# Linear attention and a highway layer on one core: all engine orders replaced, two decay factors made by products, the last pieces written another way

## The chip, the cores and the metric

One core of one Trainium2 chip runs the kernel. Its engines are TensorE (PE; its weight loads are PEld), VectorE (DVE), ScalarE (ACT), GpSimd (POOL) and SyncE (SP), which issues the loads and stores. Each engine takes its instructions in the order in which they are written and waits, in that order, for what each needs. The metric is the device time of one execution in microseconds (us), lower is better.

## The reference, cut to what matters

Inputs are q, k, v of 4 batches, 8 heads, 768 positions and 64 channels, a decay `lam` per head, two weights of 512 x 512 and a bias, all float32.

```python
for b in range(nb):                       # blocks of 64 positions, per head
    intra = (qb @ kb.T) * Dmask           # lam ** (i - j) where i >= j, else 0
    out[b] = intra @ vb + (qb * lam ** (pos + 1)) @ kv_state
    kv_state = lam ** 64 * kv_state + (kb * lam ** (63 - pos)).T @ vb
x = out.transpose(0, 2, 1, 3).reshape(3072, 512)
H = maximum(x @ w_h, 0)
T = sigmoid(x @ w_t + b_t)
result = T * H + (1 - T) * x
```

## The kernel before

The 4 x 768 positions are cut into twelve tiles n of 256 rows, three to a batch; a tile has two blocks b of 128 rows. The decay is split: v is multiplied by `lam ** -t` (`pow_v`, step CV), and the attention's result by `lam ** t` (`pow_o`, step D), so that scores need only a mask of zeros and ones (`tri`), and the state `kv` is a plain sum in PSUM. `pow_o` has three parts, one for each place of a tile in its batch, `[128, 2, 4, 128]` each; step `PW.i` makes part i, as four exponentials on ACT.

The whole order of the program is written by hand in the string `PLAN`: one token for one step, `name.tile.block...@engine=bank`. The steps:

- loads on SP, half a tile of q, k or v each (256 KB): `Lq`, `Lk`, `Lv`; the weights by `W` (half a matrix, 512 KB, `W.1` is w_t and `W.0` is w_h); stores `ST` of a tile (512 KB), in parts for the last tile
- casts to bf16: `CK`, `CQ` (a third number 2 means the whole tile, 0 or 1 a half), `CV` with the factor, `WC` of the weights
- transposes on PE (`TK`, `TQ`, `RK`, `RQ`, `RKF`, `RQF`) and their copies out of PSUM (`EK`, `EQ`, `FK`, `FQ`)
- scores `S`, state `U`, both interleaved `SA`, `SB`; mask `M` on DVE; state to bf16 `KE`; attention `A` (inside the block) and `I` (with the state); result to bf16 `D` on DVE
- the highway layer for 128 rows and 512 columns (a last number 0 or 1 means 256 columns, used for tile 11, block 1): `BP` copies the bias into a PSUM bank, `F.n.b.1` adds the gate's matmuls to it, `F.n.b.0` makes relu's input; `TX`, `TXB` transpose the rows back and `XC` copies them out as `xs`; `H` = max(h, 0) - x on DVE; `G` the sigmoid on ACT, in place in PSUM or (`@S`) into SBUF; `X` the product with the gate; `Y` the sum with x, into the output buffer `ob`
- `Z.r` runs r matmuls that only keep PE busy; `QB`, `RB` spread the bias; `PT` loads ACT's sigmoid table

Before PLAN's steps a set-up makes the identity, the masks, `ln` of the decays, `off` (ln times the start of each part, on POOL) and `pow_v`. Buffers are rings (`BUFS`: four of each load, four of `ob`, six of `y`, three of `g`); a load into a buffer waits until the last step that reads it is done, and SP holds everything behind it.

Of the kernel before, what the change touches and what calls it, by code (L numbers as in the profile page):

```python
# [21 lines left out]
Lk.2.1 WC.1.1.0@ACT WC.1.1.1@POOL S.1.0=14 D.0.1@DVE KE.0.1@ACT WC.1.0.1@POOL Lq.3.0 BP.0.1.2@DVE=0 PT F.0.0.1.2
M.1.0.1 Lq.3.1 CV.1.2@POOL M.1.1.1 TXB.0.0=3 G.0.0.2@S F.0.1.1.2 Lk.3.1 M.1.1.0 Z.2=6 M.1.0.0 G.0.1.2@S U.1.0 Lk.3.0
WC.0.1.0@POOL A.1.1=52 BP.1.0.2@DVE=0 KE.1.0@ACT TXB.0.1=4 WC.0.1.1@POOL Lv.2.1 A.1.0 BP.1.1.2@ACT=6 I.1 CQ.2.2@DVE
XC.0.2.1@ACT U.1.1 D.1.0@DVE RQF.2=1 Lv.2.0 WC.0.0.1@ACT WC.0.0.0@POOL F.1.0.1.2 EQ.2.1@DVE XC.0.2.0@ACT D.1.1@DVE
Lv.3.0 EQ.2.0@ACT F.0.1.0.2=4 CK.2.2@DVE Lv.3.1 TXB.1.1=3 TXB.1.0=5 H.0.1.2 Lq.4.0 XC.1.2.1@ACT RKF.2=1 F.0.0.0.2=2
KE.1.1@ACT X.0.1.2@POOL EK.2.1@DVE Lq.4.1 XC.1.2.0@ACT EK.2.0@DVE S.2.0=31 G.1.0.2@S H.0.0.2 Lk.4.0 CQ.3.2@POOL
S.2.1=45 F.1.1.0.2=0 M.2.1.1 Lk.4.1 CK.3.2@ACT Y.0.1.2@POOL M.2.0.1 RQF.3=5 Lv.4.1 M.2.0.0 RKF.3=2 EQ.3.1@ACT M.2.1.0
F.1.0.0.2=4 Lq.5.0 EK.3.1@ACT CV.2.2@POOL H.1.1.2 EK.3.0@ACT S.3.1=31 Lq.5.1 H.1.0.2 EQ.3.0@ACT F.1.1.1.2 M.3.1.1
BP.2.0.2@ACT=0 Lv.4.0 CV.3.2@POOL U.2.0 M.3.0.1 S.3.0=25 Lk.5.0 KE.2.0@ACT A.2.0=14 M.3.0.0 A.2.1 I.2 Lk.5.1  # L30
CQ.4.2@ACT M.3.1.0 X.0.0.2@POOL U.3.0 D.2.0@DVE Lv.5.0 A.3.1=32 G.1.1.2 A.3.0 D.2.1@DVE RQF.4=5 KE.3.0@ACT Lv.5.1
CK.4.2@POOL F.2.0.1.2 EQ.4.0@DVE X.1.1.2@DVE Lk.6.0 I.3 Y.0.0.2@POOL G.2.0.2@S RKF.4=1 EQ.4.1@DVE Lk.6.1 D.3.0@DVE
F.2.0.0.2=4 EK.4.0@ACT D.3.1@DVE Lq.6.0 CQ.5.2@POOL EK.4.1@ACT TX.2.2=56 U.3.1 XC.2.2.0@ACT Lq.6.1 S.4.1=01
Y.1.1.2@DVE CV.4.2@POOL TXB.3.0=3 XC.2.2.1@ACT RQF.5=5 M.4.0.1 Lv.6.1 KE.3.1@ACT TXB.3.1=2 F.3.0.0.2=6 H.2.0.2
XC.3.2.0@ACT Lq.7.1 EQ.5.1@ACT M.4.1.1 CK.5.2@POOL F.2.1.0.2=0 XC.3.2.1@ACT H.3.0.2 Lv.6.0 EQ.5.0@ACT X.1.0.2@POOL
BP.3.0.2@DVE=4 SA.4=3 RKF.5=1 Lq.7.0 KE.4.0@ACT M.4.1.0 F.3.0.1.2 BP.2.1.2@ACT=6 CV.5.2@POOL EK.5.1@DVE Lk.7.0
# [39 lines left out]
def kernel(  # L76
# [82 lines left out]
    for i in range(1, NST):  # L159
        P.tensor_scalar(off[:, i], in0=off[:, 0], scalar1=float(2 * C * i), scalar2=None, op0=ALU.mult)  # L160
# [313 lines left out]
```

## Time and profile before

| | before |
|---|---|
| time, median of 3 runs | 103.34 us (101.49 to 103.61) |
| profiled execution: its time, its span | 102.99 us, 101.3 us |
| PE busy | 91.9 us (91% of the span) |
| DVE busy | 85.7 us (85%) |
| POOL busy | 82.3 us (81%) |
| ACT busy | 74.5 us (74%) |
| DMA | 27.54 MB, mean 272 GB/s |
| HBM | 20.97 MB read, 6.29 MB written |

The span runs from the first to the last instruction of the profiled execution; the time of that execution has something around it. Busy time is that of instructions at work: a waiting instruction isn't counted, and the ends of matmuls are modelled, so that PE's share says least. Where a row of a group ends with "idle before", this is the time that its engine waited ahead of such instructions, and the arrow names what ended most of it. In a row of the timeline the first number is the start and the second the length, both in us.

### The profile page before, as it was taken

To read this page: it belongs to the slowest core of one execution; us is meant where nothing else is said; L and a number is where in the kernel's file an instruction comes from. 1 tells how busy PE (TensorE), PEld (TensorE's weight loads), DVE (VectorE), ACT (ScalarE), POOL (GpSimd) and SP (SyncE) were. 2 spreads that over 40 slices of the span, in tenths; PEclk is the share of its full clock that TensorE was granted. 3 is DMA by queue.
4 is the path that set the end of the run, shared out by engine and by line. 5 is a ranking of instruction groups with operands and counts; after the bars stand their busy time and mean duration, and the time that the engine had idled before them with its cause. 6 is when DMAs were issued, how large, how long until landed. Compare 5 with 4: busy or idle time off the path is not lost.

```text
span 101.3 us, 4242 instructions
## 1 busy us (share of the span) xinstructions
PE 91.9 (91%) x1784; PEld 57.0 (56%) x1803; DVE 85.7 (85%) x157; ACT 74.5 (74%) x134; POOL 82.3 (81%) x83
## 2 busy tenths in 40 slices
PE   5999999999889998999999897999999999999910
PEld 1445566565547764675676654685567474465700
DVE  4137749998979998999999985999899989999870
ACT  3596958886598599799898895869996673664610
POOL 6734557732969999998799998999899999999830
PEclk9999999999999999999999999999999999999995
DMA  0999999999999999999999999999999105009683
GB/s 22 309 300 311 357 338 365 366 340 302 254 292 306 338 300 290 299 271 304 283 288 288 319 314 395 392 310 279 294 392 364 36 6 201 6 21 366 239 307 112
DMA packets 33335, 27.54 MB, mean 272 GB/s; under 512 B 1443, under 2 KB 26275, under 8 KB 33316
## 3 DMA queue, kind: packets, MB, share of 16 engines
q1 hardware_dynamic: 33312, 27.27, 87.4%
q8 instruction: 14, 0.23, 1.0%
q14 instruction: 5, 0.04, 0.2%
q10 hardware_dynamic: 4, 0.00, 0.0%
HBM read 20.97 MB, written 6.29 MB: 269 GB/s over the span
## 4 chain that ended last, share of the span: by engine, by line
PE 31%; DMA 29%; SPq 10%; POOL 7%; DVE 7%; issue 7%; ACT 5%; DVEq 0%; POOLq 0%; ACTq 0%
DMA kf<-in_k_dram 14%; PE bt L378 9%; PE bh L378 9%; DMA w_f<-in_moe_w_h_dram 8%; DMA qf<-in_q_dram 7%; SPq L198 5%; SPq L194 4%; PE kv L267 2%; PE bs L262 2%; POOL ob L404 2%; POOL kb L113 2%; DVE y L391 2%; POOL vs L221 2%; PE bo L335 2%; SPq L202 2%
## 5 line engine op out<-in xcount | busy, mean ns | idle before, releaser
L304 DVE TENSOR_TENSOR m<-bs,tri 128x512 bf16<-128x512 f32 x48 | 31.0, 681 | 1.2 <-PE kv L267 1.0
L221 POOL TENSOR_TENSOR vs<-vf,pow_v 128x1024 bf16<-128x1024 f32 (+1 forms) x13 | 23.4, 1805 | 5.1 <-DMA vf<-in_v_dram 3.1
L378 PEld LDWEIGHTS <-xT 128*128 128x128 bf16 x200 | 17.7, 98 | 16.8 <-DVE xT L341 0.3
L404 POOL TENSOR_TENSOR ob<-y,xs 128x512 f32<-128x512 bf16 x21 | 24.3, 1173 | 0.6 <-DVE y L400 0.4
L378 PE MATMUL bh<-w_b,xT 128*128 128x512 bf16 (+1 forms) x93 | 23.8, 370 | 0.5
L378 PE MATMUL bt<-w_b,xT 128*128 128x512 bf16 (+1 forms) x89 | 23.1, 370 | 1.1 <-issue 0.3
L400 POOL TENSOR_TENSOR y<-g,y 128x512 bf16<-128x512 f32 x15 | 17.3, 1159 | 2.7 <-DVE y L391 2.6
L391 DVE SCALAR_TENSOR_TENSOR y<-bh,xs 128x512 bf16<-128x512 f32 (+1 forms) x25 | 16.3, 660 | 1.8 <-PE bh L378 1.8
L341 DVE TENSOR_TENSOR xT<-bo,pow_o 128x512 bf16<-128x512 f32 x24 | 15.6, 679 | 0.1
L111 ACT ACTIVATE ss<-kv 128x512 bf16<-128x512 f32 x19 | 11.4, 601 | 3.9 <-PE kv L267 3.8
L396 ACT ACTIVATE g<-bt 128x512 f32<-128x512 f32 x15 | 9.0, 602 | 5.0 <-PE bt L378 4.4
L111 ACT ACTIVATE bt<-b_bc 128x512 f32<-128x512 f32 (+1 forms) x20 | 11.5, 580 | 1.4 <-DVE xT L341 0.6
L262 PE MATMUL bs<-qT,kT 64*64 64x128 bf16 x384 | 11.5, 220 | 0.0
L111 ACT ACTIVATE xs<-bx 128x512 bf16<-128x512 bf16 x15 | 9.0, 604 | 1.3 <-PE bx L354 0.8
L262 PEld LDWEIGHTS <-kT 64*64 64x64 bf16 x384 | 8.2, 106 | 2.7 <-DVE kT L113 1.2
L267 PE MATMUL kv<-vs,kb 64*64 64x64 bf16 x320 | 8.6, 194 | 0.2 <-POOL vs L221 0.2
L267 PEld LDWEIGHTS <-kb 64*64 64x64 bf16 x320 | 7.0, 109 | 3.0 <-issue 2.0
L335 PE MATMUL bo<-m,vs 64*64 64x128 bf16 x384 | 8.5, 218 | 0.0
L418 PE MATMUL bspin<-blank,id 128*128 128x512 bf16 x26 | 8.3, 444 | 0.1
L113 POOL CAST kb<-kf 128x1024 bf16<-128x1024 f32 (+1 forms) x7 | 6.8, 976 | 1.5 <-DMA kf<-in_k_dram 1.5
L396 ACT ACTIVATE bt<-bt 128x512 f32<-128x512 f32 (+1 forms) x10 | 5.5, 546 | 2.4 <-PE bt L378 2.4
L335 PEld LDWEIGHTS <-vs 64*64 64x64 bf16 x384 | 6.4, 107 | 0.6
(67 smaller groups left out, 133.2 us busy)
## 6 DMA issues: line engine op xcount, KB each, us to landing
...
```

The source lines that it names most:

```text
L111: A.activation(dst, src, AF.Copy)
L221: ENG[eng].tensor_tensor(buf("vs", n)[:, hs], in0=buf("vf", n)[:, hs].rearrange("p h (j d) -> p h j d", j=J), in1=pow_v[:, n % NST, hs, :, ...
L262: T.matmul(get("s", n, e, hp // 2)[half(b), hp % 2, j, :], lhsT=buf("kT", n)[half(e), hp, j, half(b)], rhs=q_cols(n, half(e), hp, b), star ...
L267: T.matmul(kv[half(e), hp, half(e)], lhsT=buf("kb", n)[half(b), j, 2 * hp + e, :], rhs=buf("vs", n)[half(b), 2 * hp + e, j, :], start=firs ...
L304: V.tensor_tensor(buf("m", n, e, u), in0=get("s", n, e, u), in1=tri[:, None].to_broadcast([128, 2, J, C]), op=ALU.mult)
L335: T.matmul(get("o", n, b)[half(e), hp, :], lhsT=buf("vs", n)[half(b), 2 * hp + e, j, :], rhs=buf("m", n, e, hp // 2)[half(b), hp % 2, j, : ...
L341: V.tensor_tensor(cut(buf("xT", n)[:, :, b * C:(b + 1) * C]), in0=get("o", n, b).rearrange("e k (j p) -> e k p j", j=Q), in1=cut(pow_o[:, ...
L378: T.matmul(t, lhsT=buf("xT", n)[:, j, b * C:(b + 1) * C], rhs=w_b[w][:, j, z], start=(j == 0 and not w), stop=(j == KC - 1), skip_group_ch ...
L391: V.scalar_tensor_tensor(buf("y", n, b)[:, z], in0=get("h", n, b, p), scalar=0.0, in1=buf("xs", n)[:, b, z], op0=ALU.max, op1=ALU.subtract)
L396: A.activation(buf("g", n, b)[:, cols(p)] if to == "S" else t, t, AF.Sigmoid)
L400: ENG[eng].tensor_tensor(y, in0=buf("g", n, b)[:, cols(p)] if eng == "POOL" else get("t", n, b, p), in1=y, op=ALU.mult)
L404: ENG[eng].tensor_tensor(buf("ob", n)[:, b, z], in0=buf("y", n, b)[:, z], in1=buf("xs", n)[:, b, z], op=ALU.add)
```

## The change

Three things are changed.

1. `PLAN` is another order of all engines. On SP: `Lk` of tile 0 comes first, both halves of `Lv.1` stand ahead of the four `W` (before: behind the first two), `Lv.2` ahead of `Lq.3` and `Lk.3`, `ST.1` and `ST.2` between the loads of tiles 9 to 11, and `ST.4` behind `ST.6`. There are 20 `Z` matmuls in place of 27. Steps that change engine:

```
to DVE from POOL: CK.1.2 CK.5.2 CV.0.1 X.0.1 X.8.0
to DVE from ACT:  CK.3.2 CK.11.2 KE.1.1 PW.1 PW.2 BP.1.1 BP.3.1 BP.11.0 BP.11.1.0
                  EK.0.1 EK.3.1 EQ.1.0 EQ.3.1 FK.6.0 FK.6.1 FK.9.0 FQ.7.0 FQ.9.0 FQ.10.1
                  XC.0.0 XC.2.0 XC.2.1 XC.3.1 XC.7.0 XC.7.1
to POOL from DVE: CK.0.1 CQ.2.2 X.1.1 X.2.1 X.3.0 X.7.1 Y.1.1
to POOL from ACT: CK.8.2 CQ.4.2 WC.0.0.1 WC.1.1.0
to ACT from POOL: CK.4.2 CK.7.2 CK.9.2 CK.10.2 CQ.0.1 CQ.3.2 CQ.5.2 CQ.8.2 WC.0.0.0 WC.1.0.1
to ACT from DVE:  CQ.0.0 CQ.1.2 BP.0.1 BP.1.0 BP.3.0 BP.6.0 BP.9.1
                  EK.0.0 EK.2.1 EQ.0.1 EQ.2.1 EQ.4.0 FK.10.1 FQ.6.0 FQ.7.1 FQ.9.1 FQ.10.0 FQ.11.0 FQ.11.1
                  XC.4.1 XC.5.1 XC.10.0 XC.10.1 XC.11.0
```

2. Parts 1 and 2 of `pow_o` are products of part 0 with a factor per head, `grown`, on DVE; four plus four exponentials on ACT go, one small one comes.
3. The last two pieces (tile 11, block 1, 256 columns each) are computed as relu(h) g + (1 - g) x: `GN` makes 1 - g as a second sigmoid, `R` its product with x, `HG` relu(h) times g, and `Y` sums the two. Before they were g (relu(h) - x) + x.

```diff
 PLAN = """
-Lk.0.0 Lq.0.0 Lq.0.1 Lk.0.1 Lv.0.1 Lq.1.0 Z.9=5 Lq.1.1 PW.0@ACT CQ.0.0@DVE Lv.0.0 CK.0.0@POOL Lk.1.0 Lk.1.1
-CQ.0.1@POOL TK.0.0=2 W.1.0 PW.2@ACT Z.1=5 TQ.0.2=3 CK.0.1@DVE W.1.1 Z.1=5 TK.0.1=4 EQ.0.0@DVE QB=6 EQ.0.1@DVE Lv.1.0
-CV.0.1@POOL EK.0.0@DVE EK.0.1@ACT Lv.1.1 S.0.0=01 RB@ACT S.0.1=53 CQ.1.2@DVE Lq.2.1 Z.3=4 PW.1@ACT M.0.0.0 RQF.1=2
...
-Y.10.0.2@POOL F.11.1.0.0=5 G.11.0.2 TXB.11.1=3 F.11.1.1.0 X.11.0.2@DVE XC.11.2.1@ACT ST.10 F.11.1.0.1=0 G.11.1.0
-H.11.1.0 F.11.1.1.1 Y.11.0.2@POOL H.11.1.1 X.11.1.0@DVE G.11.1.1 X.11.1.1@DVE ST.11.0.2 Y.11.1.0@DVE Y.11.1.1@DVE
-ST.11.1.0 ST.11.1.1
+Lk.0.1 Lk.0.0 Lq.0.1 Lq.0.0 Lv.0.0 Lv.0.1 Z.5=1 Lq.1.0 PW.0@ACT Lq.1.1 CK.0.1@POOL Lk.1.0 CK.0.0@POOL Lk.1.1 TK.0.1=2 TK.0.0=3
+PW.2@DVE Lv.1.0 CQ.0.1@ACT Z.6=1 Lv.1.1 CQ.0.0@ACT PW.1@DVE EK.0.0@ACT TQ.0.2=4 W.1.1 Z.3=1 EQ.0.1@ACT EK.0.1@DVE CV.0.0@POOL
+Z.1=3 W.1.0 EQ.0.0@DVE PT S.0.1=60 S.0.0=15 CV.0.1@DVE W.0.1 QB=3 M.0.1.0 U.0.0 Z.2=4 W.0.0 CQ.1.2@ACT KE.0.0@DVE Lq.2.0
...
+F.11.1.1.0 F.11.1.0.0=6 XC.11.2.1@ACT X.11.0.2@DVE F.11.1.1.1 ST.10 G.11.1.0@S GN.11.1.0 F.11.1.0.1=5 Y.11.0.2@POOL
+HG.11.1.0 GN.11.1.1 R.11.1.0@DVE G.11.1.1@S R.11.1.1@DVE HG.11.1.1 ST.11.0.2 Y.11.1.0@DVE Y.11.1.1@DVE ST.11.1.0 ST.11.1.1
 """
...
+    grown = singles.tile([128, NST, NP], F32)
+    A.activation(grown[:, 1:], off[:, 1:], AF.Exp)
...
+    rest = singles.tile([C, DM], F32)
+    part = singles.tile([C, DM], F32)
+    parted = set()
...
-    def powers(i):
+    def powers(i, eng):
+        if eng != "ACT":
+            ENG[eng].tensor_tensor(pow_o[:, i], in0=pow_o[:, 0], in1=grown[:, i, None, :, None].to_broadcast([128, 2, NP, C]), op=ALU.mult)
+            return
...
+    def sigm_rest(n, b, p):
+        A.activation(rest[:, cols(p)], get("t", n, b, p), AF.Sigmoid, scale=-1.0)
+
+    def kept(n, b, p, eng):
+        z = cols(p)
+        ENG[eng].tensor_tensor(rest[:, z], in0=rest[:, z], in1=buf("xs", n)[:, b, z], op=ALU.mult)
+
+    def gated(n, b, p):
+        z = cols(p)
+        V.scalar_tensor_tensor(part[:, z], in0=get("h", n, b, p), scalar=0.0, in1=buf("g", n, b)[:, z], op0=ALU.max, op1=ALU.mult)
+        parted.add((n, b, p))
...
     def total(n, b, p, eng):
         z = cols(p)
-        ENG[eng].tensor_tensor(buf("ob", n)[:, b, z], in0=buf("y", n, b)[:, z], in1=buf("xs", n)[:, b, z], op=ALU.add)
+        last = (n, b, p) in parted
+        ENG[eng].tensor_tensor(buf("ob", n)[:, b, z], in0=part[:, z] if last else buf("y", n, b)[:, z],
+                               in1=rest[:, z] if last else buf("xs", n)[:, b, z], op=ALU.add)
```

More of the change, by code (lines that the diff above doesn't have):

```diff
@@ L22 @@
[L22 to L36, printed above, removed]
@@ L429 @@
         "KE": lambda a, e, bk: evac_s(*a, e), "M": lambda a, e, bk: mask(*a),
-        "I": lambda a, e, bk: inter(*a, bk), "A": lambda a, e, bk: intra(*a, bk), "D": lambda a, e, bk: take(*a, e), "PW": lambda a, e, bk: powers(*a), "QB": lambda a, e, bk: spread(bk), "RB": lambda a, e, bk: copy(e, b_bc, get("qb")),
+        "I": lambda a, e, bk: inter(*a, bk), "A": lambda a, e, bk: intra(*a, bk), "D": lambda a, e, bk: take(*a, e), "PW": lambda a, e, bk: powers(*a, e), "QB": lambda a, e, bk: spread(bk), "RB": lambda a, e, bk: copy(e, b_bc, get("qb")),
         "TX": lambda a, e, bk: rows(*a, bk), "TXB": lambda a, e, bk: rows_full(*a, bk),
```

35 lines of the change are left out of this document (2 added, 33 removed).

## The prediction, made before the changed kernel ran

> **What bounds the kernel now.** I read the busy line and the chain of the page first, then busy time by stretch, then the groups by form, then the timeline around single rows. In the first fence the reader is to see that four engines are nearly full, and that the chain which ended last is spread over all of them.
>
> ```profile
> PE 91.9 (91%) x1784; PEld 57.0 (56%) x1803; DVE 85.7 (85%) x157; ACT 74.5 (74%) x134; POOL 82.3 (81%) x83
> ...
> PE 31%; DMA 29%; SPq 10%; POOL 7%; DVE 7%; issue 7%; ACT 5%; DVEq 0%; POOLq 0%; ACTq 0%
> ```
>
> The stretches (columns: stretch, its length, then busy us and count of PE, PEld, DVE, ACT, POOL; granted clock; DMA share; GB/s) say where each engine has room.
>
> ```profile
> 0.00:10.10 10.10, 8.86 (x68) 4.17 (x69) 4.30 (x12) 6.57 (x14) 5.72 (x19) 1.00 0.78 235
> 10.10:15.00 4.90, 4.85 (x72) 2.93 (x74) 3.17 (x6) 3.88 (x9) 2.79 (x4) 1.00 1.12 349
> 15.00:30.00 15.00, 13.95 (x268) 8.59 (x259) 13.34 (x24) 11.69 (x21) 9.22 (x10) 1.00 1.08 323
> 30.00:95.00 65.00, 62.64 (x1386) 40.15 (x1395) 62.08 (x111) 50.92 (x91) 62.75 (x51) 1.00 0.87 266
> 95.00:101.30 6.30, 1.59 (x17) 1.20 (x14) 2.85 (x7) 1.48 (x4) 1.77 (x2) 0.79 0.59 212
> ```
>
> From 30 to 95 us, of 65.0 us, DVE is busy 62.08, POOL 62.75, PE 62.64 and ACT 50.92. A long stall of one engine is not there to be removed. DVE from 15 to 95 us is busy 13.34 + 62.08 = 75.42 of 80, so its waits are 4.6 us. Before 10.1 us it works only 4.30. DMA is behind this:
>
> ```profile
> 66.39 4.44 SPq L198 DMA_DIRECT2D vf<-in_v_dram  x4
> 70.87 25.15 SPq L408 DMA_DIRECT2D out_dram<-ob  x9
> ```
>
> The last four loads (tile 11's v among them) are issued by 70.83 us and the queue then holds only stores; 30 us of compute follow. So I take DVE as the bound: its end is its start, plus its work, plus its waits, with PE and POOL close behind. The span is 101.3 us, the profiled execution 102.99 us (1.69 us lie around the span); the median of the runs is 103.34 us, 0.35 more, and the runs go from 101.49 to 103.61, so that about 2% is what a measurement here can tell from no change.
>
> **The change part by part.** Prices, by operation and shape (mean ns of one is the number after the comma):
>
> ```profile
> L304 DVE TENSOR_TENSOR m<-bs,tri 128x512 bf16<-128x512 f32 x48 | 31.0, 681 | 1.2 <-PE kv L267 1.0
> ...
> L221 POOL TENSOR_TENSOR vs<-vf,pow_v 128x1024 bf16<-128x1024 f32 x11 | 21.3, 1943 | 2.8 <-DMA vf<-in_v_dram 1.9 <-DVE m L304 0.5 <-DMA qf<-in_q_dram 0.4
> L400 POOL TENSOR_TENSOR y<-g,y 128x512 bf16<-128x512 f32 x15 | 17.3, 1159 | 2.7 <-DVE y L391 2.6
> L113 POOL CAST kb<-kf 128x1024 bf16<-128x1024 f32 x6 | 6.2, 1038 | 1.5 <-DMA kf<-in_k_dram 1.5
> ...
> L346 ACT ACTIVATE pow_o<-t_f,off 128x256 f32<-128x256 f32 x12 | 5.7, 559 | 0.0
> L400 DVE TENSOR_TENSOR y<-bt,y 128x512 bf16<-128x512 f32 x8 | 5.4, 681 | 0.3 <-ACT bt L396 0.3
> L111 ACT ACTIVATE qb<-qf 128x1024 bf16<-128x1024 f32 x5 | 5.3, 1052 | 2.0 <-DMA qf<-in_q_dram 2.0
> ...
> L111 ACT ACTIVATE kb<-kf 128x1024 bf16<-128x1024 f32 x4 | 4.2, 1060 | 1.2 <-DMA kf<-in_k_dram 1.2
> ...
> L113 DVE COPY xs<-bx 128x512 bf16<-128x512 bf16 x9 | 3.6, 412 | 0.4 <-POOL ob L404 0.4
> L113 DVE COPY bt<-b_bc 128x512 f32<-128x512 f32 x5 | 3.4, 682 | 0.0
> ...
> L404 DVE TENSOR_TENSOR ob<-y,xs 128x512 f32<-128x512 bf16 x2 | 2.1, 1064 | 0.0
> ...
> L113 DVE CAST qb<-qf 128x512 bf16<-128x512 f32 x1 | 0.9, 887 | 0.7 <-DMA qf<-in_q_dram 0.7
> ...
> L404 DVE TENSOR_TENSOR ob<-y,xs 128x256 f32<-128x256 bf16 x2 | 0.7, 416 | 0.0
> L113 DVE CAST kb<-kf 128x1024 bf16<-128x1024 f32 x1 | 0.7, 694 | 0.4 <-DMA kf<-in_k_dram 0.4
> ...
> L113 DVE CAST kb<-kf 128x512 bf16<-128x512 f32 x1 | 0.4, 427 | 1.5 <-DMA kf<-in_k_dram 1.5
> ...
> L152 DVE TENSOR_TENSOR p_ln<-ln,tk_f 128x48 f32<-128x48 f32 x1 | 0.2, 209 | 1.4 <-ACT ln L150 1.4
> ```
>
> *Shared-port work.* DVE steps with two SBUF inputs, or SBUF to SBUF casts, have met POOL three times. In the rows below ob of 512 takes 0.84 and 1.29 where 0.681 is the time of such an operation; the half cast qb took 0.887 against 0.427 for kb:
>
> ```profile
> 36.59 0.84 DVE L404 TENSOR_TENSOR ob<-y,xs 128x512 f32<-128x512 bf16 x1
> 88.84 1.29 DVE L404 TENSOR_TENSOR ob<-y,xs 128x512 f32<-128x512 bf16 x1
> ```
>
> and POOL was held at the same two places (1.90 and 1.16 are its usual times):
>
> ```profile
> 36.84 2.35 POOL L221 TENSOR_TENSOR vs<-vf,pow_v 128x1024 bf16<-128x1024 f32 x1
> 89.67 1.49 POOL L404 TENSOR_TENSOR ob<-y,xs 128x512 f32<-128x512 bf16 x1
> ```
>
> So a meeting costs DVE 0.16 to 0.61 and POOL 0.3 to 0.4. Y.1.1's goes with the step (counted below); Y.8.0's 0.61 goes if its place is free: -0.61. But after 15 us the new order has five such steps on DVE (CK.2.2, 3.2, 5.2, 11.2, Y.8.0) beside a POOL that is 97% busy. Nothing but the order of each engine keeps them apart. Bounds: 0, and five times a whole vs product, 1.9. I take two meetings at 0.45, a middle price and what qb paid: +0.9.
>
> The Trainium skill, page "SBUF — State Buffer", section "Who interferes with whom", states that this pair of ports is an exclusive lock: whichever of the two engines starts first keeps it for its whole instruction. The rows agree: POOL's 2.35 row begins under DVE's 0.84 row and ends 0.44 late. Taken at its word, a cast that meets a fresh vs product would wait up to 1.9 us, and two such would be 3.8 for my 0.9; that is a rival below.
>
> *DVE after the start.* I counted the steps of both orders by engine. Leaving DVE: the cast CQ.2.2 (0.70, as the kb cast of that size, 0.694), five bias copies BP (5 x 0.682 = 3.41), four gates X (4 x 0.681 = 2.72), the two half gates of the last pieces (0.84 together, at the half ob's 0.416), Y.1.1 (0.84). Coming: casts CK.1.2, 3.2, 5.2, 11.2 (4 x 0.694 = 2.78), three BP and a half one (2.05 + 0.42), KE.1.1 (0.69, as a cast), two gates X (1.36), two half products R (0.84 together). Fifteen 0.41 us copies out of PSUM leave and fifteen come. 8.51 go, 8.14 come: -0.37 us. The H steps of the last pieces become HG at the same form.
>
> *Two decay factors as products.* Eight of the twelve exponentials leave ACT: 8 x 5.7/12 = -3.8 us. DVE gets two products of 1024 elements from two SBUF inputs. Not shown before: between 0.694 (the 1024-element cast) and 1.94 (the product of that size on POOL). From 48 elements in 0.209 and 512 in 0.681 a product costs 1.02 ns per element, so 1024 take 1.20; I take that, 2.4 in all. The first 10 us of DVE change by CQ.0.0, CQ.1.2, CK.0.1 and two copies leaving (0.89 + 0.70 + 0.43 + 0.83 = 2.85) and products, CV.0.1 (0.68) and one copy coming (3.5): +0.65, beside 5.8 idle us there.
>
> ```profile
> 4.41 3.67 ACT L346 ACTIVATE pow_o<-t_f,off 128x256 f32<-128x256 f32 x8
> 4.47 0.42 POOL L160 TENSOR_SCALAR off<-off 128x4 f32<-128x4 f32 x2
> ...
> 10.10 1.88 DVE L304 TENSOR_TENSOR m<-bs,tri 128x512 bf16<-128x512 f32 x3
> ```
>
> A wait is added: the new little exponential `grown` needs `off`, ready at 4.89, and stands ahead of PW.0 on ACT, which began at 4.41. With about 0.2 for `grown`, PW.0's four exponentials (3.67/8 = 0.46 each) end near 6.9 in place of 6.25. Queued behind are CQ.0.1, CQ.0.0, EK.0.0 and EQ.0.1 on ACT, and on DVE both products, EK.0.1, EQ.0.0, CV.0.1 and the first mask. Products end at 6.9 + 2.4 = 9.3, CV.0.1 and two copies later it is 10.8; the first mask ran at 10.10. So +0.7, at worst +1.7 with a port wait. DVE is idle 1.7 us in the 4.9 us after that (3.17 busy), which a later start eats first, and I count the start at 0; without that cover it is the 0.7.
>
> *Loads.* SP now takes both halves of v1 ahead of the four w loads (512 KB each), and v2 ahead of q3 and k3. The second half of w_t comes two 256 KB units later, 0.52 MB at the 349 GB/s of 10 to 15 us = 1.5 us.
>
> ```profile
> 16.28 0.82 PE L378 MATMUL bt<-w_b,xT 128*128 128x512 bf16 x3 [0.17 <-DVE xT L341]
> ```
>
> The first gate block, 16.28 us, moves to about 17.8 on PE; v1 comes four units, 3 us, earlier, so that the attention of tile 1 fills PE meanwhile. I cost it at nothing; uncovered it is 1.5. Stores: ST.1 and ST.2 now stand ahead of the last loads. Lv.11 waits on SP behind ST.2, thus for Y.2.1 on POOL and for one more 512 KB, 1.5 us at that rate; with 30 us left after the last load this costs nothing. ST.4 goes behind ST.6; Y.8 reuses its buffer only after five more POOL steps (over 6 us). Fewer warming matmuls (20 for 27) are no work on the path.
>
> *Tail.* Before, the last matmul group is the gate's, and sigmoid, gate and sum follow:
>
> ```profile
> 95.99 0.60 PE L378 MATMUL bt<-w_b,xT 128*128 128x256 bf16 x4
> ...
> 96.62 0.83 DVE L400 TENSOR_TENSOR y<-bt,y 128x256 bf16<-128x256 f32 x2
> 96.63 0.37 ACT L396 ACTIVATE bt<-bt 128x256 f32<-128x256 f32 x1 [0.44 <-PE bt L378]
> ...
> 97.37 0.75 DVE L404 TENSOR_TENSOR ob<-y,xs 128x256 f32<-128x256 bf16 x2
> ```
>
> From 96.59 it takes a sigmoid to 97.00, a gate to 97.45 and the sum to 98.12. After, relu's block is last; the sigmoid has begun one half block (0.43, four of its 256-wide matmuls) earlier, but GN precedes it (0.3). HG and two sums follow: 1.3 for 1.5. -0.2 us; R reads two SBUF inputs beside POOL's Y.11.0, which may take it back.
>
> *POOL and ACT.* POOL: five CK, one CQ (1.04 each) and CV.0.1 (1.04) fewer, two X (1.16) and one Y (taken as an X) more: -3.8 us. ACT: -3.8 for the exponentials, three CQ (1.05), one CK (1.06), two half CQ (half of 1.05 and a little, 0.6), one BP (taken as DVE's, 0.7), two half sigmoids GN (0.37) and `grown` more: about +3.2. From 15 to 95 us ACT is busy 11.69 + 50.92 = 62.6 of 80; 5 more fit.
>
> *Waits of DVE.* The order is new, so its 4.6 us of waits are drawn anew. Where before packs well, they are small:
>
> ```profile
> 30.00:40.00 10.00, 9.63 (x228) 6.70 (x224) 9.51 (x17) 8.33 (x16) 9.96 (x8) 1.00 1.12 305
> 40.00:50.00 10.00, 9.74 (x210) 5.80 (x211) 9.67 (x18) 8.96 (x16) 9.42 (x8) 1.00 1.01 292
> 50.00:60.00 10.00, 9.67 (x255) 6.70 (x256) 10.00 (x19) 8.82 (x16) 9.33 (x8) 1.00 1.02 295
> ```
>
> 0.49, 0.33 and 0.00 us in three tens, 0.27 in the mean; at that rate 80 us would have 2.2, a gain of 2.4. Lighter POOL speaks for some of it, fuller ACT against. Bounds -2.4 and +2.4; I take half the gain, -1.2.
>
> Sum: -0.37 - 0.61 + 0.9 - 0.2 - 1.2 = -1.5 us: 102.99 - 1.5 = **101.5 us**, in its own range 100.3 to 102.6.
>
> **The rivals.**
>
> *Good packing.* No new meetings and all of the 2.4: -0.37 - 0.61 - 0.2 - 2.4 = -3.6, 99.4 us. For it: POOL, 97% full, gets 3.8 us of room, and so every gate waits less. Against: PE's 62.64 of 65 has the same work.
>
> *PE or the balance binds.* PE's matmuls of the tiles are untouched; if it ends last in most stretches, DVE's saved work turns into waits: 102.99, call it 103.0. For: PE is the largest share of the chain, 31%. Against: its ends are modelled, so its share overstates.
>
> *Casts meet POOL.* The other side. The five steps after 15 us meet POOL, at 0.75 each, between the 0.61 measured and half a vs product, 0.95: 3.8 us; PW.1 or CV.0.1 meets CV.0.0 at the start and the first mask is 1.7 late with no cover. -0.37 - 0.2 + 3.8 + 1.7 - 0.6 (Y.8.0's own, paid already) = +4.3, but POOL's -3.8 gives back a share of its waits, 1.2: 106.1 us. It loses from about three meetings at the long price on. For: POOL is 97% full; both steps of 512 elements after 30 us met it. Against: five POOL casts fewer leave gaps. The exclusive lock on the page named above is this rival's mechanism.
>
> *The order does not do what it says.* Loads come at other moments than planned, the new order waits for w_t (1.5) at the head of PE and saves nothing else: 104.1.
>
> **How the numbers follow.** Forecast 0.42, good packing 0.26, PE binds 0.15, casts 0.11, late loads 0.06. Within the forecast's case some 0.4 lies more than 2% below the median (101.27), so faster is 0.26 + 0.16 = 0.42; over 105.4 lies the casts' case and a little of the last, 0.12; same 0.46. The range of 8 in 10 is 98.8 to 104.4: it takes in most of the fast case and the late loads, and leaves out the casts.
>
> **What would show it.** Right: DVE's sum about 85 us, POOL's near 78, ACT's near 78; kb casts on DVE at 0.69; first mask between 10 and 11 us; pow_o products near 1.2 us each; POOL's 2.35 row gone. Wrong: kb casts on DVE over 1 us, DVE waits over 5 us between 15 us and the end, or a first gate block after 19 us. A forecast of no net gain would show as PE full and DVE idle.

## The result: 3.4% slower, and the profile after

The changed kernel takes 105.74 us (median of 6 runs, 105.05 to 107.35), the kernel before 102.84 us on the same chip (6 runs, 101.49 to 103.61): a ratio of 1.034, with an interval from 1.025 to 1.044. The profiled execution took 105.05 us, its span is 103.3 us: 2.0 us over the 101.3 before. The forecast was 101.5. Medians are over all runs; ratios and their intervals are over the runs within 1.5% of a kernel's fastest, so that the two can differ.

The busy line and the shares of the chain that ended last, of the kernel after:

```profile
PE 91.3 (88%) x1778; PEld 56.8 (55%) x1796; DVE 90.0 (87%) x156; ACT 76.7 (74%) x136; POOL 79.4 (77%) x79
...
PE 76%; DVE 13%; issue 4%; ACT 3%; DVEq 0%; ACTq 0%
```

The reader is to see the last line first. Before, PE had 31% of the chain beside DMA's 29%; now the chain lies on PE for 76% of the span. POOL and ACT came out as counted (79.4 and 76.7 for "near 78"); DVE has 90.0 where the prediction had about 85.

Busy time by stretch, kernel after, same stretches as before (stretch, length, PE, PEld, DVE, ACT, POOL, clock, DMA share, GB/s):

```profile
0.00:10.10 10.10, 8.86 (x53) 4.22 (x53) 4.42 (x10) 6.07 (x13) 6.71 (x19) 1.00 0.78 244
10.10:15.00 4.90, 4.00 (x74) 2.23 (x66) 4.25 (x6) 3.86 (x6) 1.99 (x2) 1.00 1.10 385
15.00:30.00 15.00, 13.14 (x237) 8.24 (x240) 13.87 (x24) 9.03 (x18) 8.83 (x10) 1.00 1.07 352
30.00:95.00 65.00, 62.20 (x1399) 39.91 (x1413) 62.73 (x111) 54.94 (x95) 59.03 (x48) 1.00 0.77 250
95.00:103.30 8.30, 3.06 (x29) 2.15 (x25) 4.71 (x9) 2.79 (x7) 2.88 (x3) 1.00 0.54 203
```

And three tens of them:

```profile
30.00:40.00 10.00, 9.14 (x220) 6.47 (x221) 9.42 (x17) 7.73 (x14) 9.16 (x8) 1.00 1.02 312
40.00:50.00 10.00, 8.67 (x197) 5.63 (x197) 9.77 (x16) 8.46 (x15) 7.10 (x7) 1.00 1.04 311
50.00:60.00 10.00, 9.84 (x230) 6.61 (x232) 9.76 (x19) 9.40 (x17) 10.00 (x9) 1.00 1.07 348
```

DVE is busy 13.87 + 62.73 = 76.60 of the 80 us from 15 to 95, so it waits 3.4 us: the prediction's 4.6 - 1.2, to the tenth. That term came true, and the kernel is slower. (The agreement is luck: the term was half of a bound that ran both ways, and time in which GpSimd holds up a step of VectorE counts as busy here and not as a wait.) What got worse is PE: 4.00 for 4.85 between 10.1 and 15 us, 13.14 for 13.95 between 15 and 30, 8.67 for 9.74 between 40 and 50. From 50 us on it is as full as a profile shows it.

The groups that the prediction priced (after; mean ns of one is the number after the comma):

```profile
L61 DVE CAST kb<-kf 128x1024 bf16<-128x1024 f32 x5 | 6.6, 1314 | 0.0
...
L299 DVE TENSOR_TENSOR pow_o<-pow_o,grown 128x1024 f32<-128x1024 f32 x2 | 2.4, 1222 | 2.6 <-ACT pow_o L302 2.6
...
L174 POOL TENSOR_TENSOR vs<-vf,pow_v 128x512 bf16<-128x512 f32 x1 | 2.1, 2090 | 1.9 <-DMA vf<-in_v_dram 1.9
...
L359 DVE TENSOR_TENSOR rest<-rest,xs 128x256 f32<-128x256 f32 x2 | 1.4, 747 | 0.0
```

A product is 1.22 us (1.20 predicted). A k cast on VectorE is 1.31 in the mean, not 0.69: four of the five were held up by POOL, at 1.63, 1.07, 1.03 and 2.16, and each of the four ends 0.55 us after POOL's instruction does. The fifth, at 75.58, took 0.68. POOL was held too: a half vs product takes 2.09 beside the products, for 1.04 before, a weight cast at 14.85 takes 1.07 beside the first of the k casts, for 0.61, and a gate at 75.80 takes 1.47 beside the fifth, for 1.16. The longest meeting, in the timeline (start, us, engine):

```profile
42.45 1.91 POOL L174 TENSOR_TENSOR vs<-vf,pow_v 128x1024 bf16<-128x1024 f32 x1
...
42.74 2.16 DVE L61 CAST kb<-kf 128x1024 bf16<-128x1024 f32 x1
...
44.96 0.62 PE L186 MATMUL bktr<-id,kb 128*128 128x128 bf16 x8 [1.22 <-DVE kb L61]
```

VectorE's cast of tile 5 starts 0.29 us after POOL's vs product and ends 0.55 after it; PE stands 1.22 us for its k transposes. The Trainium skill, page "SBUF — State Buffer", section "Who interferes with whom", has the later engine wait for the whole instruction of the earlier; these two rows agree (1.91 - 0.29 = 1.62 at most, and the cast took 1.47 more than alone).

The first gate block on PE, and the last of the weight casts that it needs, on ACT:

```profile
20.51 0.60 PE L334 MATMUL bt<-w_b,xT 128*128 128x512 bf16 x2
```

```profile
19.04 0.63 ACT L59 ACTIVATE w_b<-w_f 128x512 bf16<-128x512 f32 x1
```

It was 16.28 before and forecast at about 17.8. And the last pieces:

```profile
97.46 0.60 PE L334 MATMUL bh<-w_b,xT 128*128 128x256 bf16 x4
97.58 1.15 POOL L373 TENSOR_TENSOR ob<-y,xs 128x512 f32<-128x512 bf16 x1 [0.78 <-DVE y L368]
...
97.92 1.42 DVE L359 TENSOR_TENSOR rest<-rest,xs 128x256 f32<-128x256 f32 x2
...
99.27 0.41 DVE L363 SCALAR_TENSOR_TENSOR part<-bh,g 128x256 f32<-128x256 f32 x1
99.60 0.74 DVE L373 TENSOR_TENSOR ob<-part,rest 128x256 f32<-128x256 f32 x2
```

From the start of the last matmul group to the end of the last sum it is 97.46 to 100.34, 2.88 us, and before 95.99 to 98.12, 2.13: 0.75 longer. The two R steps (97.92, 1.42 for both, the first 1.08 beside POOL's 97.58 row) hold up the second gated piece until 99.27, though its matmuls end at 98.06 and its sigmoid at 98.38.

So the 2.0 us of the span are about 1.5 us that PE comes late to its last group (97.46 for 95.99) and 0.75 us behind it, less what the last store does.

**How PE's lag was followed.** A busy PE is not a PE at its peak, so matmuls were counted by work: each at its spacing behind the one before (a single 512-column matmul is 0.38 us, two are 0.59 and four 1.03, so 0.216 each), and summed from a moment to the end. The plan says how many each step has; 17 or 18 records of the gate and relu blocks are missing in most traces and were filled in. Both kernels have 81.9 us of such work, the warming matmuls left out. What is left of it, in us (the six rows below the second are runs of the next section):

```
                     at 20   30    45    50    65    95   last group starts
before                74.3  65.5  50.5  46.0  31.6   1.4   95.99
after                 75.8  66.5  53.7  48.6  33.2   2.9   97.46
products on old       75.2  65.9  51.7  46.9  31.6   1.4   96.04
new loads on old      75.7  67.3  52.6  47.5  32.1   2.8   97.52
old to 32 us, new     74.6  65.0  52.4  47.0  31.8   1.7   96.31
new to 26 us, old     75.9  67.3  53.2  48.4  33.2   3.0   97.66
after, more warming   77.0  68.2  54.4  50.5  35.1   4.8   99.41
after, products undone 78.5 70.2  57.3  53.1  38.0   7.3  101.94
```

The weights are an estimate, and the level hangs on them: from 30 to 95 us the kernel before does 65.5 - 1.4 = 64.1 us of matmul work by them, but 58.5 if each kind of matmul is taken at its spacing inside an unbroken group. The differences between the rows depend on them less: by either count the changed kernel is 1.5 us behind at 20 us and 1.5 at 95.

Between these two moments the lag is not constant. Of the seven kernels under the first row, four are as late at the last group as at 20 us, to 0.2 us; the two last rows lose more on the way (2.7 to 3.4, 4.2 to 6.0), and products on old has lost its lag by 65 us. And new loads on old is only 0.5 us behind at 65 us, and 1.4 again at 95. That a late start simply stays is therefore the theory that fits best, and not a thing that the table shows at each step.

How full PE is, is better read where no matmul record is missing. In tail_undone (the new order, see below), from 50 to 95 us:

```profile
50.00:95.00 45.00, 44.98 (x997) 27.77 (x996) 43.51 (x80) 39.33 (x69) 42.71 (x35) 1.00 0.63 210
```

By its busy time PE has nothing to spare there; what a little less of its work brings is tried below (after_less_pe). In the old order, a profile with all records (less_dve, below) has 1.25 us of idle PE from 30 to 95 us, where the busy time of before, with records missing, had said 2.4.

### The profile page after: what moved, and what is told of

Same layout as the page of the kernel before. It is cut to its first block, busy times and chain, and to the rows that moved or that the text cites. A ratio compares the mean times of both kernels' runs of the same rounds, so it can differ in the third digit from the quotient of the medians.

```text
span 103.3 us, 4234 instructions
## 1 busy us (share of the span) xinstructions
PE 91.3 (88%) x1778; PEld 56.8 (55%) x1796; DVE 90.0 (87%) x156; ACT 76.7 (74%) x136; POOL 79.4 (77%) x79
## 4 chain that ended last, share of the span: by engine, by line
PE 76%; DVE 13%; issue 4%; ACT 3%; DVEq 0%; ACTq 0%
PE bt L334 19%; PE bh L334 18%; PE bs L215 6%; PE bo L288 6%; PE bspin L388 5%; DVE kb L61 5%; PE bo L277 4%; DVE m L257 4%; PE bktr L186 4%; PE kv L220 3%; PE bx L310 3%; PE btr L202 3%; PE cold L77 1%; PE bx L319 1%; PE bqtr L186 1%
## 5 line engine op out<-in xcount | busy, mean ns | idle before, releaser
L368 POOL TENSOR_TENSOR y<-g,y 128x512 bf16<-128x512 f32 x17 | 20.0, 1181 | 9.3 <-DVE y L347 3.9
L373 POOL TENSOR_TENSOR ob<-y,xs 128x512 f32<-128x512 bf16 x22 | 25.2, 1161 | 2.3 <-DVE y L368 2.0
L334 PE MATMUL bt<-w_b,xT 128*128 128x512 bf16 (+1 forms) x91 | 23.6, 370 | 0.6 <-DVE m L257 0.2
L347 DVE SCALAR_TENSOR_TENSOR y<-bh,xs 128x512 bf16<-128x512 f32 x23 | 15.5, 682 | 0.7 <-ACT xs L59 0.3
L59 ACT ACTIVATE bt<-b_bc 128x512 f32<-128x512 f32 (+1 forms) x21 | 12.3, 597 | 1.6 <-DVE xT L294 1.4
L352 ACT ACTIVATE g<-bt 128x512 f32<-128x512 f32 (+1 forms) x19 | 11.1, 584 | 2.4 <-PE bt L334 2.4
L59 ACT ACTIVATE xs<-bx 128x512 bf16<-128x512 bf16 x14 | 7.9, 596 | 2.5 <-PE bx L310 1.7
L59 ACT ACTIVATE qb<-qf 128x1024 bf16<-128x1024 f32 (+1 forms) x10 | 9.6, 972 | 0.0
L59 ACT ACTIVATE qT<-bqtr 128x512 bf16<-128x512 bf16 x10 | 6.0, 612 | 3.4 <-PE bqtr L186 3.4
L59 ACT ACTIVATE kT<-bktr 128x512 bf16<-128x512 bf16 x9 | 5.3, 594 | 4.2 <-DVE kT L61 4.1
```

Of the source, the lines that this page charges most:

```text
L59: A.activation(dst, src, AF.Copy)
L334: T.matmul(t, lhsT=buf("xT", n)[:, j, b * C:(b + 1) * C], rhs=w_b[w][:, j, z], start=(j == 0 and not w), stop=(j == KC - 1), skip_group_ch ...
L347: V.scalar_tensor_tensor(buf("y", n, b)[:, z], in0=get("h", n, b, p), scalar=0.0, in1=buf("xs", n)[:, b, z], op0=ALU.max, op1=ALU.subtract)
L352: A.activation(buf("g", n, b)[:, cols(p)] if to == "S" else t, t, AF.Sigmoid)
L368: ENG[eng].tensor_tensor(y, in0=buf("g", n, b)[:, cols(p)] if eng == "POOL" else get("t", n, b, p), in1=y, op=ALU.mult)
L373: ENG[eng].tensor_tensor(buf("ob", n)[:, b, z], in0=part[:, z] if last else buf("y", n, b)[:, z], in1=rest[:, z] if last else buf("xs", n) ...
```

## The experiments

Two theories stood after the result. **Meetings**: VectorE's casts and POOL hold each other up. **Start**: PE gets its first work of the highway layer late, and since it is full afterwards, the delay stays. The edits are shown in the words of the plan.

**The casts.** First the four moved casts went back to the engines that they had, then all five to ACT, then the old order got the change's engines:

```diff
 casts_undone (changed kernel)
-CK.1.2@DVE CK.3.2@DVE CK.5.2@DVE CK.11.2@DVE
+CK.1.2@POOL CK.3.2@ACT CK.5.2@POOL CK.11.2@ACT
 casts_act (changed kernel): CK.1.2, 2.2, 3.2, 5.2, 11.2
-@DVE
+@ACT
 old_casts_dve (kernel before)
-CK.1.2@POOL CK.3.2@ACT CK.5.2@POOL CK.11.2@ACT
+CK.1.2@DVE CK.3.2@DVE CK.5.2@DVE CK.11.2@DVE
```

> The changed kernel with CK.1.2 and CK.5.2 back on POOL and CK.3.2 and CK.11.2 back on ACT, as they were before; all else as changed. Theory 'port meetings' (casts on DVE that meet POOL: 1.63, 1.03, 2.16 and 0.68 us where 0.69 is the time of such a cast, 2.7 us too much, and PE waits 2.6 us for kb): 2 to 3 us below the changed kernel, 102.5 to 103.7. Theory 'start' (the new order brings the first gate block to PE 4.2 us later and PE does not get it back): within 0.7 us of the changed kernel, 105 to 106.4, since four casts cost the other engines as much. Theory 'balance' (POOL and ACT become the bound with the casts): no gain or slower, 105.5 to 107.

Measured: 106.85 us (106.42 to 107.26), 1.046 [1.035, 1.056].

> The changed kernel with all five kb casts of whole tiles that it has on DVE (CK.1.2, 2.2, 3.2, 5.2, 11.2) on ACT. 'Port meetings': DVE loses 6.6 us of work (3.1 of it waiting for the port), ACT gains 5 x 1.05; 2 to 4 us below the changed kernel, 101.7 to 103.7. 'Start': 105 to 106.5. 'Balance' (ACT full): ACT at 82 us, its copies late, 105 to 107.

Measured: 105.77 us, 1.032 [1.015, 1.050].

> The kernel before with only the four casts CK.1.2, 3.2, 5.2 and 11.2 moved to DVE, in the old order. 'Port meetings': DVE gets 4 x 0.69 of work and at least two meetings of 0.4 to 1.5 each, while POOL loses 2.1: 1.5 to 4 us above the kernel before, 104.3 to 106.8. 'Start' (casts on DVE are harmless): 102.3 to 103.8, the bare 2.8 us partly taken up by DVE's waits.

Measured: 105.92 us (105.0 to 106.5), 1.037 [1.021, 1.053]. Its group of k casts:

```profile
L113 DVE CAST kb<-kf 128x1024 bf16<-128x1024 f32 x5 | 5.6, 1113 | 0.4 <-DMA kf<-in_k_dram 0.4
```

The price is real: in the old order the four casts on VectorE, 2.8 us of plain work and 2.1 us of meetings (1.11 for 0.69 in the mean of five), cost as much as the whole change; the run does not tell the two apart. But in the new order nothing comes back when the casts are moved away. With the casts on ACT, PE still waits for tile 5's, because the cast now stands in ACT's queue (PE rows of casts_act):

```profile
44.17 0.62 PE L186 MATMUL bktr<-id,kb 128*128 128x128 bf16 x8 [0.44 <-ACT kb L59]
```

That is 0.79 us earlier than after, and yet PE's last group starts at 98.25, later than after's 97.46. A fourth kernel left tile 11's cast, which had not been held up, where it was:

```diff
 casts_four_act (changed kernel): CK.1.2, 2.2, 3.2, 5.2
-@DVE
+@ACT
```

> The changed kernel with the casts of k of tiles 1, 2, 3 and 5 on ACT in place of VectorE, and that of tile 11, which met nothing there, left on VectorE. With all five on ACT, PE had 0.9 us less work left than the changed kernel at 45 us and lost it again between 75 and 80 us, where tile 11's cast was the one moved. Theory that the four meetings cost what PE lost there: 104.6 to 105.0, 0.5 to 1 us under the changed kernel. Rival, that the new order stalls at these steps whoever casts: 105.5 to 106.

Measured: 105.55 us (104.86 to 107.5), 1.034 [1.023, 1.045]. The rival held: the new order is as slow whoever casts, and taking the four meetings away does not take the 3.4% away. Whether ACT's queue then costs what the meetings had cost is not told apart.

**The products.**

```diff
 products_undone (changed kernel)
-PW.2@DVE ... PW.1@DVE
+PW.2@ACT ... PW.1@ACT
```

> The changed kernel with PW.1 and PW.2 as four exponentials each on ACT again, at the same places. 'Port meetings': the two products cost DVE 2.4 us before its first mask, where it had nothing else; ACT's exponentials hold CQ.0.1 and CQ.0.0 by 1.8 us instead, so the start gets later: 105.3 to 107.5. 'Start, through the products' (the products hold EK.0.1, EQ.0.0, CV.0.1 on DVE and one meets CV.0.0, 2.09 us for 1.04): 0.5 to 1.5 us below the changed kernel, 104.2 to 105.2.

Measured: 109.97 us (109.32 to 110.35), 1.077 [1.064, 1.089]. The first mask of this kernel:

```profile
15.30 0.68 DVE L257 TENSOR_TENSOR m<-bs,tri 128x512 bf16<-128x512 f32 x1
```

It was 10.69 after. 4.6 us at the start, and the last group on PE starts 4.5 us later (101.94 for 97.46): a delay at the start, with a halved clock in it (below), is there at the end. In matmul work PE is 2.7 us behind the changed kernel at 20 us and 4.5 at 50. In the old order the products do no harm:

```diff
 old_products (kernel before, with the new code of the products)
-PW.2@ACT ... PW.1@ACT
+PW.2@DVE ... PW.1@DVE
```

> The kernel before with one part of the change, the two decay factors as products on VectorE at the same places of the order. PW.2 frees ACT of about 2 us near 6 to 8 us, PW.1 of 2 us at 10 us, for 1.2 us each of VectorE, which is idle 5.8 us in the first 10. Theory of matrix progress: if the first evacuations of tile 0 and 1 come earlier, PE is ahead by up to 1 us at 20 us and the time is 102 to 103; if the products block VectorE ahead of the first masks, 103.5 to 104.5. Without any effect on PE's progress: 103.3.

Measured: 102.46 us against 102.72 (10 and 19 runs), 1.003 [0.998, 1.008]: no difference. PE is 0.9 us behind at 20 us here and level at 65; the old order took this delay up.

**Where along the kernel.** The two orders were joined at moments where they have done nearly the same steps.

```diff
 old_to_i2: every engine's steps in the old order up to I.2, the rest in the new one
 old_to_m5: the same up to M.5.1.0 and F.3.1.1.2
 new_to_m5: the new order up to M.5.0.1, the rest in the old one
 new_to_q2: the new order up to EQ.2.1, the rest in the old one
```

> The old order, products and all, of every engine up to the last masks of tile 5 (about 46 us), then the rest in the new order with the new last pieces. Theory that matrix progress up to 45-50 us sets the time (the changed kernel has 3.2 us more matrix work left at 45 us than before, and wins 1.2 back later): the loss goes, 101 to 103 us, PE's idle between 10 and 50 us as before. Rival, that port meetings and the new last pieces set it: three of the five meetings and CV.0.0's go too, but the late ones (CK.11.2, R) stay, so 103 to 104.5. Rival, that the whole new order is slower at every place: 104 to 105.

Measured: 103.52 us, 1.010 [1.005, 1.016]. At the seam, one gate of tile 2 (`X.2.1` on POOL) reads its factor from a buffer that its sigmoid, still the old one, does not write, at the same cost.

> The old order of every engine up to the second half of tile 2's attention (about 32 us), then the new order. Theory of matrix progress: of the 3.2 us that the changed kernel lags at 45 us, 1.0 had gathered by 30 us; that part goes, the part of tile 5's late cast stays if CK.5.2 meets POOL again: about 104, between the changed kernel and the one that is old up to 46 us. If the start alone is the cause: 103 or less, as the other.

Measured: 104.24 us (104.06 to 104.31), 1.016 [1.008, 1.024]. Of this the profile has 0.3 us in PE's last group (96.31) and 0.75 behind it, with the new last pieces. So the start is not the whole: with the old start, 1.0% and 1.6% are left, and "103 or less" did not come.

> The other way round: the new order with its products and loads up to tile 5's masks (about 48 us), then the old order and the old last pieces. Ten PSUM banks differ, since the two orders have them in other places there. Theory of matrix progress: the loss is made by 48 us and stays, 105 to 106.5. Rival, that the late part of the new order and the last pieces lose: 103 to 104.

Measured: 107.19 us, 1.035 [1.021, 1.050]. In this kernel one gate of tile 2 is multiplied without its sigmoid, at the same cost.

> The new order of every engine with products and loads up to tile 2's first evacuations (about 26 us), then the old order and the old last pieces; five PSUM banks differ. The changed kernel has 1.0 to 1.5 us more matrix work left than before between 20 and 30 us. Theory that a late start passes to the end: 104 to 104.8. Rival, that the old order takes it up, as it took up a lag of 0.9 us at 20 us when it was given the products alone: 102.7 to 103.3.

Measured: 105.01 us against 102.96, 1.029 [1.015, 1.042]. The joined plan leaves out no step, but its result is off by 9%, and why is not known; its times are those of the same steps in this order. The new order's first 26 us alone cost most of what the whole change costs, and behind them the old order, which is fast by itself, does not make it good: PE's last group starts at 97.66, later even than after. The parts do not add up to the whole (2.9% for the start and 1.6% for the rest, for 3.4%).

One of the four meetings lies inside this start. In the changed kernel PE stands 0.95 us for the k cast of tile 1, the one of 1.63 us:

```profile
15.51 0.62 PE L186 MATMUL bktr<-id,kb 128*128 128x128 bf16 x8 [0.95 <-DVE kb L61]
```

**What binds.** 5.3 us of VectorE's work or 4.3 us of PE's were left out of both kernels:

```diff
 less_dve, after_less_dve: mask(n, e, u), for n > 1 and u == 1
-    V.tensor_tensor(m, in0=s, in1=tri)            # 512 elements
+    V.tensor_tensor(m[:, 0:1], in0=s[:, 0:1], ...)  # 256
 less_pe, after_less_pe: block(n, b, w, p), for n > 1 and w == 1
-    for j in range(KC):
+    for j in range(KC - 1):
```

> The kernel before with two of the four masks of each tile from tile 2 on cut to half their columns (the other half of m keeps old data): 20 masks of 512 elements at 0.681 become masks of 256, at 0.416 as the other 256-element rows, so VectorE has 5.3 us less work and all else is the same. Theory that VectorE is the bound, as the prediction had it: 4 to 5 us faster, about 98.5. Theory that PE's progress sets the time: under 1 us faster, 102 to 103. Both in turn: 100 to 101.5.

Measured: 102.8 us against 102.85 in the medians, ratio 0.990 [0.981, 0.999].

> The kernel before with one of the four accumulating matmuls of each gate block left out from tile 2 on: 19 whole blocks and two half ones, 20 matmuls of 512 at 0.216 between starts, so PE has 4.3 us less work and all else is the same. Theory that PE's progress sets the time: 3 to 4.3 us faster, 99 to 100. Theory that VectorE is the bound: under 1 us, 102 to 103. Both in turn: 100.5 to 102.

Measured: 102.47 us, 0.994 [0.986, 1.002].

Neither gave what its theory asked. The busy line of less_dve, and its stretch from 30 to 95 us, where DVE has 58.71 in place of 62.08:

```profile
PE 92.0 (91%) x1803; PEld 56.5 (56%) x1803; DVE 81.2 (81%) x157; ACT 74.8 (74%) x134; POOL 82.4 (82%) x83
```

```profile
30.00:95.00 65.00, 63.75 (x1403) 40.55 (x1402) 58.71 (x112) 51.60 (x92) 63.17 (x51) 1.00 0.88 269
```

VectorE has 3.4 us more air in these 65 than before, and PE, whose records are complete here, is busy 63.75: it has little room to follow. (The 1803 in the first of these lines are the same matmuls as the 1784 before; so many records were missing there.) In the old order, then, neither PE nor VectorE binds alone. That work taken from one runs into the other is argued, since no run took from both; POOL, busy 63.17 of the 65, is a rival that no run tested.

> The changed kernel with 20 masks from tile 2 on cut to half their columns (the rest of m keeps old data), 5.3 us of VectorE work, as was done to the kernel before. Theory that PE binds from 50 us on: the masks of tiles 2 to 5 come earlier and give back some of what PE loses up to 45 us, 0.5 to 1.2 us, about 104.7. Rival, that VectorE's work is the bound: 4 us or more, 101.5. Rival, that both bind in turn: 103 to 104.

Measured: 105.24 us (104.73 to 105.52), 1.031 [1.020, 1.043]: 0.5 us under the changed kernel's median, within the intervals. From 50 to 95 us, first after, then without the masks' halves:

```profile
50.00:95.00 45.00, 44.39 (x989) 27.81 (x999) 43.55 (x80) 38.75 (x68) 42.77 (x35) 1.00 0.66 222
```

```profile
50.00:95.00 45.00, 44.42 (x988) 27.72 (x998) 41.63 (x80) 38.66 (x68) 42.58 (x35) 1.00 0.67 225
```

DVE falls from 43.55 to 41.63 and PE stays at 44.4 of 45.

> The changed kernel with one of four accumulating matmuls of each gate block left out from tile 2 on, 4.3 us of PE work, as was done to the kernel before. Theory that in the new order PE is full from 50 us on and what is late at 50 us is late at the end: 2 to 4 us faster than the changed kernel, 102 to 103.5. Rival, that the new order is tied up across engines as the old one is (0.6 us there): 105.

Measured: 103.48 us (100.9 to 103.92), some 2.3 us under the changed kernel in the medians; the slowest of these four runs is below the fastest of the changed kernel's (105.05). In the new order PE binds first, and VectorE doesn't: this is what the theory of PE's progress said, at the lower end of its range. Of the 4.3 us taken, about half came back.

**The last pieces.**

```diff
 tail_undone (changed kernel; order of the last matmul groups kept)
-G.11.1.0@S GN.11.1.0 ... HG.11.1.0 GN.11.1.1 R.11.1.0@DVE G.11.1.1@S R.11.1.1@DVE HG.11.1.1
+G.11.1.0 ... H.11.1.0 G.11.1.1 X.11.1.0@DVE H.11.1.1 X.11.1.1@DVE
```

> The changed kernel with the old form of the last pieces (relu minus x, gate, sum; the order of the last matmul groups stays the new one). In the changed kernel the second gated piece waited on VectorE from about 98.5 to 99.27 behind a product R that ran 1.08 us beside POOL, where 0.41 is its time alone. Theory: the form of the last pieces costs the 0.7 us of that meeting, and the time falls by 0.6 to 1.0 to about 104.8. Rival, that the saved step of the new form is worth what the meeting takes: 105.5, no change.

Measured: 105.54 us (105.19 to 105.91), 1.036 [1.030, 1.042]: no change. In the profiles the stretch from the last group's start to the last sum's end is 98.79 to 101.21, 2.42, for 2.88 after: 0.46 us less, which the medians do not show. This profile's PE was later than that of after before it came there (its last group starts 1.3 us later), so how much of the 0.46 is in the time stays open.

**The clock and the warming.** In five profiles of kernels with the new start (casts_undone, products_undone, tail_undone, casts_four_act, new_to_m5; in a sixth, after_old_loads, 3.4 us before 12 us) the granted clock fell to a half for 3.4 us, or for 6.8 us in products_undone and new_to_m5, between 12 and 21 us; with the old start it stayed at 1.00 there (old_to_m5 apart, whose profiled execution ran at half clock throughout and is not used). The worst, products_undone:

```profile
15.00:20.00 5.00, 4.63 (x54) 3.45 (x55) 4.21 (x7) 2.27 (x5) 4.70 (x7) 0.50 1.08 385
```

```diff
 after_warm (changed kernel): warming matmuls before four steps of PE
+Z.4 RKF.1 ... Z.1 S.1.0 ... Z.1 U.1.0 ... Z.1 F.0.1.1.2
```

> The changed kernel with seven warming matmuls more (27, as many as before) at the four places between 13 and 20 us where PE waited: four ahead of the k transposes of tile 1, one each ahead of its scores, its first state update and the first gate block. At full clock each takes 0.216, into waits of 0.95, 0.3, 0.4 and 0.3 us. Theory of the clock: in the new start PE waits enough that the granted clock falls to a half for 2 to 6 us in some executions; the warming keeps it at 1.00, the median falls by 0.4 to 0.8 us to about 105.1 and the runs over 106 go. Rival, that the clock is only a sign of the late start: no change, 105.6.

Measured: 106.48 us (105.68 to 106.99), 1.041 [1.026, 1.057]. The clock was 1.00 throughout this profile, and the kernel was no faster. Three of the four places:

```profile
14.50 1.67 PE L440 MATMUL bspin<-blank,id 128*128 128x512 bf16 x6 [0.30 <-DVE m L309]
17.44 0.39 PE L440 MATMUL bspin<-blank,id 128*128 128x512 bf16 x1
19.72 0.39 PE L440 MATMUL bspin<-blank,id 128*128 128x512 bf16 x1 [0.87 <-DVE m L309]
```

The warming is in the way: the k transposes of tile 1 start at 16.32 for 15.51, and the matmul at 19.72 waits 0.87 us for a mask to free its PSUM bank, where the state update behind it had no wait. PE is 1.2 us further behind at 20 us and 1.95 us at its last group. So this run doesn't price the clock. Nor do the executions of one kernel: the changed kernel's with the lowest mean clock (0.966) was its longest, 107.35, but tail_undone took 105.19 at 0.974 and 105.31 at 1.000. But the profiles of after, casts_act and new_to_q2 have the loss at a full clock, and the clock is not its cause.

**The loads.** Last, each kernel got the other's order of the first 28 loads, its engines left as they were.

```diff
 old_new_loads (kernel before); after_old_loads (changed kernel) the other way round; behind the loads of tile 0's k and q
-... Lv.0.1 Lq.1.0 Lq.1.1 Lv.0.0 Lk.1.0 Lk.1.1 W.1.0 W.1.1 Lv.1.0 Lv.1.1 Lq.2.1 W.0.1 Lq.2.0 W.0.0 ...
+... Lv.0.0 Lv.0.1 Lq.1.0 Lq.1.1 Lk.1.0 Lk.1.1 Lv.1.0 Lv.1.1 W.1.1 W.1.0 W.0.1 W.0.0 Lq.2.0 Lq.2.1 ...
```

> The kernel before with the changed kernel's order of the first 28 loads (both halves of tile 1's v ahead of the four weight loads, tile 2's v ahead of tile 3's q and k), its engines in the old order. Theory that the order of the loads makes the start late: the first gate block waits for the second half of w_t, up to 1.5 us, and it passes to the end: 103.5 to 104.4. Theory that the engines' own order makes it late: under 0.5 us, 102.5 to 103.3.

Measured: 104.0 us (103.05 to 104.65, 6 runs) against 103.03, 1.021 [1.010, 1.032]. POOL and PE of this kernel:

```profile
16.95 1.74 POOL L113 CAST w_b<-w_f 128x512 bf16<-128x512 f32 x3 [3.31 <-DMA w_f<-in_moe_w_t_dram]
```

```profile
17.62 0.38 PE L378 MATMUL bt<-w_b,xT 128*128 128x512 bf16 x1 [0.55 <-POOL w_b L113]
18.74 0.59 PE L378 MATMUL bt<-w_b,xT 128*128 128x512 bf16 x2 [0.74 <-POOL w_b L113]
```

```profile
97.52 0.60 PE L378 MATMUL bt<-w_b,xT 128*128 128x256 bf16 x4
```

POOL stands 3.31 us for w_t; PE's first gate block begins at 17.62, where the prediction had put it, and stops twice, 0.55 and 0.74 us, for the casts. The lag of 1.4 us at 20 us is 1.5 at the last group: 97.52, within 0.1 of the changed kernel's 97.46. In between it had fallen to 0.5 at 65 us (the table above), and why it came back is open.

> The changed kernel with the old order of the first 28 loads. Its first gate block ran at 20.51, behind a cast of w_b that ACT began at 19.04 behind its own queue, while the weights had been cast by POOL from 14.85 on. Theory that the loads make the start late: 104 to 104.8. Theory that the engines' order does: the weights come earlier and wait, tile 1's v comes later, 105.3 to 106.2.

Measured: 109.38 us (108.54 to 110.09), 1.077 [1.069, 1.086]. Neither theory had this. POOL waits 4.52 us for tile 1's v in this kernel and the first mask runs at 13.82: the new order of the engines is bound to its loads, so what each of the two costs in the changed kernel cannot be had by exchanging one of them.

## Why the prediction was wrong, by its own steps

- **"So I take DVE as the bound."** This is the step that failed. Without 5.3 us of VectorE's work the old order gains 1.0% and the new one nothing that the intervals tell; without 4.3 us of PE's the old one gains 0.6%, which the interval does not tell from nothing, and the new one some 2.3 us. Every term that was a change of VectorE's work or waits (-0.37, -0.61, +0.9, -1.2, together -1.3) was therefore not in the time, though the waits came out right, by luck. The prediction set PE aside for "its ends are modelled"; in the new order, with all records, PE was busy 44.98 of 45 us from 50 us on (tail_undone).
- **"I cost it at nothing; uncovered it is 1.5"** (loads). The mechanism, the place (17.8, run at 17.62 with the loads alone) and the uncovered price were right and the cover was not there: in the old order these loads cost 1.6 us of the span (102.9), 1.0 us in the medians and 1.021 as a ratio, of the change's 1.034. The cover named was tile 1's attention on PE; with the old order of the engines PE reached the gate block first, and in the changed kernel the block stood behind tile 1's attention in PE's order, its last cast done at 19.67, and ran at 20.51. The rival of 104.1 had this wait at the head of PE; with these loads and nothing else new it came to 104.0.
- **"I count the start at 0."** The first mask was right (10.69, within 10 to 11). The idle time of VectorE was taken for cover; the delay that counts is PE's (1.5 us of matmul work at 20 us). With its first mask 4.6 us later (products_undone), the new order came 4.5 us later to PE's last group.
- **"Two meetings at 0.45."** There were five on VectorE (four casts and R) and three on POOL; the casts alone had 3.1 us in place of 0.9, nearer to the rival "casts meet POOL". Its price shows in the old order (1.037, with the casts' own 2.8 us in it). But its 106.1 is near the measured 105.74 by chance, as far as these runs show: moved away, the casts bring nothing back.
- **The last pieces, -0.2.** They took 0.75 us more. The prediction named the meeting of R with Y.11.0 that "may take it back"; it missed that both R steps stand ahead of the second HG.
- **Right**: Y.8.0's meeting gone (0.68 now), products 1.22, POOL and ACT. Two of the signs named for "wrong" came, k casts over 1 us (1.31) and a first gate block after 19 us (20.51). Of the sign for no gain, a full PE came and an idle VectorE did not: it is busy 43.55 of the 45 us from 50 on.

Put together with the trace: loads and start 1.5 for 0, last pieces 0.75 for -0.2, and no gain from VectorE's 1.3, makes about +2.2 for the -1.5 forecast; 2.0 were measured in the spans. What the runs show of the cause is its place (most of it in the first 26 us, and the last pieces in the profiles) and, in the new order, that PE has no room from 50 us on to make a delay good. What stays open is which step of the new start costs how much, since its loads and its engine order can't be exchanged singly, why the old order takes up 0.9 us of delay with the products but not the 1.4 us of the loads, and what the late part of the new order adds (1.6% behind an old start, about 0.5% behind a new one). No version ran that beats both kernels: the old order with the products is level with before.
